# Last chunk of an FFT mixing layer: output transform in two halves of its channels, all its blocks summed in SBUF, three groups of zero matmuls, and a new order of the work

## The chip, the cores and the metric

The kernel runs on one core of a Trainium2 chip. The metric is device time in microseconds (us), as the median of several executions. A profile records one further execution: what each engine did and what it waited for. TensorE is PE (its weight loads PEld), VectorE DVE, ScalarE ACT, GpSimd POOL; SyncE, SP, issues most of the DMA transfers.

## What is computed

A layer over 2048 positions and 640 channels, all float32: a gated blend of a long causal convolution (A) and a spectral filter (B).

```python
def _A_ref(q, k, v, shift_k, ssm_k, ssm_D):
    ...                                   # k_shift: causal convolution of k with 4 taps
    kv = k_shift * v
    L = 2 * S
    ...                                   # kv_f, kf_f: FFTs of length L of kv and of ssm_k
    y_f = kv_f * kf_f[None, :, :, :]
    y = irfft2(y_f, s=(1, L))[:, 0, :S, :]
    y = y + kv * ssm_D[None, None, :]
    return q * y

def _B_ref(x, w_r, w_i):
    X = rfft2(x, axes=(-2, -1)) * (w_r + 1j * w_i)
    return irfft2(X, s=(S, D), axes=(-2, -1))

x = A_q
g = sigmoid((x * gate_w).sum(-1, keepdims=True))
return g * _A_ref(...) + (1 - g) * _B_ref(x, ...)
```

## The kernel before

All Fourier transforms are matmuls with constant matrices, so PE does most of the work; every stage of it is followed by a move out of PSUM on DVE, ACT or POOL. The 2048 positions are held as 128 partitions by 16 blocks n, the 640 channels (permuted) as five chunks c of 128.

**B, the spectral part.** x comes in 16 tiles (L342, "a<-xT"). `fold` (L347 to L358) adds and subtracts quarter tiles on DVE or POOL, with a small copy on ACT (L355). `dfwd` transforms two blocks at a time over the channels (L371, L377), and ACT copies the result into XX (L387 to L394). Then come the transform over positions, first stage `b1` (L437, transposed back by L440), second stage `bs2` (L456) with the filter product (L468, L470) and its sums (L476), and the first inverse stage `i1` (L314 on XX, transposed by L319). The rest is `bfin`, for two blocks at a time: the last inverse stage over positions (L498, L506), a copy (L517), the inverse over channels with the constant "dic" (L525, L530), ACT's scaling by 1 - g (L547 to L550), a combination on DVE (L553), and three sums and differences (L555, L556) that give the 640 output channels of a block.

**A, for each chunk.** `kv` convolves with the taps (L592 and L595, or L601 and L609) and multiplies by v (L632) after eight transposes on PE (L624). The first FFT stage is `s1` (L649, transposed by L652), once for the filter ("a", loaded as h) and once for kv. `amid` is the second stage and the product (L685, then L694, L696, L700, L702); for chunks 2, 3 and 4 its complex parts are summed by `asum` (L709). `is1a` is the first inverse stage in two halves of 64 channels (L314 on ZZ, transposed by L319). `afin` ends a chunk for eight blocks at a time: q is loaded and multiplied by g on ACT (L733), sixteen matmuls over all 128 channels give the last inverse stage (L744), DVE multiplies by q (L751).

**Joining A and B.** For chunks 0 to 3 `afin` writes its eight blocks to the output (L764), and `bout` later adds the spectral part with accumulating DMAs that POOL issues (L570). For the last chunk two ways are used. In blocks 0 to 7, `bout` writes the spectral part first (L568) and `afin` accumulates onto it (L762). In blocks 8 to 15 (`KEEP = (1,)`) the spectral part stays in a buffer of SBUF; POOL adds (L758) and SP writes (L760).

**What sets the order.** Every operation is registered with `op`, with its dependences, buffers and alternatives of engine (`either`). A table of numbers, `TABLE`, gives the order: "51+1/2/3" runs operation 51 in its second alternative, with buffer slots 2 and 3. The engines work through their own instructions in that order, and the numbers of buffers are fixed: eleven "a", five "s", eight banks of PSUM. PE starts with 24 matmuls on a zeroed tile, "wrm" (L773).

Of the kernel before, what the change touches and what calls it, by code (L numbers as in the profile page):

```python
# [25 lines left out]
KEEP = (1,)  # L26
ADDS = {}

TABLE = """
57/0 0 1/0 3 5 2 50/1 145/2 331/0 138/3 339/4 36/5 94/6 58+1/0/1 30/7 101/8 59+1 62/1 61+1 79/9 63 60<61 6 51+1/2/3 55/2 52+1 53+1 56 54+1 146+1/4/0  # L30
64/4/6 150/3 147<146 151 148 149 139/2/4 332/0 333 334 71 143/2 65 66 67 140 340+1 70 144 69 335/10 341/6/0 68 142 141 37/1/3 38 323/0 343/2 72/0
345/1 152/4/0 41 336/2 39 344 40+1<39 167/3 160/4 123/5 342 31+1/2/1 32 35 159 328/7 34 153 33 155 102+1/0/4 154 42+1/2/6 106/0 157 103+1 16/8 105+1
158 156 107 104+1 95+1/2/0 324/0 96+1 116/6 49 80+1/1/3 98+1 48 325 99/4 43 81<98 97 46 10/9 100 45 326 44 108/6/4 47 82 83 84/2 85 73+1/2/1 346 77/3
74+1 75<74 78 349/2 327/0 109 115 168/0/4 110 111 347/4 114 350 76 433/1 113 112 348 405/0 169 86+1/0/2 172/6 225/3 9/0 171 173 170+1 161+1/2/0 162+1
165/7 163+1 219/4 329/4/0 8 124+1/1/3 93 245/0 337/2 164<124 166 87 330 290/10 88 4 125 92 90 338 89 126 174/6/4 91 128/0 129 251/5 127 427/7
117+1/2/1 121/1 118+1 119+1 120+1 351/2/1 181 17/0/4 18 122 19+1<18 21 130/4/0 352 20+1 175 176 11/2/0 177 407/2 178 12 180 15 179 13 409/6 136 131
133 134 132 14 22+1/2/6 137 135 353/0 23 29 27 25 28 357/4 24 355/6 26 184/2 358 406/8 356 411/9 408<14 354 192/4 193 416/0 413/2 410 188/6 182 186/0
189 183 412 185 375/4 187 379/6 383/2 376/1 380/6 377 363/0 378 384/3 381+1 190/4 386 364/9 385 365+1 194/2 191 428+1 382+1 429/4/2 195 366+1 417/6
371/6 372/9 430 434+1 246/2 247/2/0 220/0 204/4 374+1 248 221/4/1 373+1 420/0 418/9 437/2 222 7 249 232/4 202/6 438 250 205 414/0/0 419 203 226/2
359/4 415 227/8 224 264/9 360/3 228/0/2 223 422/2 361 229 493/0 362 435/6 200/0 395/1 231 252/2 436 233/4 230 253/3 201 421 387/6 254/1/4 367/0  # L40
234/3/0 235 388/8 368/2 494/0 198/2 258/4 370 390+1 369 431/4 495/7 196/0 389 432 255<389 496 497/8 303/3 284/5 199 197 499/7 498+1 396 393/4 237<498
504/0 424/8 236 423 391/0 500 394 265/4 400/2 285/6 392 501/7 286/2/0 425/0 256 287 397/2 257 426 266/6 267/3/1 288 506/5 289 259/6 515/8 401 398 268
304/0 439/4/1 399 260/4/0 270 297/6 261 445/2 269 440 212/9 305/4 306/2/1 262 443/6 263 441/4 502/0/0 446 442 307 505/1 507 444 298/2 508/3 291/4
206/4 292/0 299/3/0 503 402/6 308 521/5 309 300 510/7 516+1 471/0 293/4/1 301 455/2 403 459/4 302 472/2 294 404 456/0 474 600/0 473 460/6 463/6 458
296 277/0 457 467/0 464/3 461+1 475/2 465 468/10 466 462 213/6 476/2 451/4 469 214/6 470 452/10 477 295<477 215/2/0 447/0 478 207/6 448/3 454+1<478
517/2/0 449 208/1/4 453+1 488/2 450 519/0 209 604/10 216 518 512/4 481/4 601/8 211+1 520 217<211 602/6 522+1 509+1 483/9 606/3 479/0 603+1 210+1 608/6
589/0 482 511<210 489 605 480 278/4 513/6 279/7 591/1 271/10 514 525/0 218 607 590/4 527/2/1 280/3/1 526 523/6 238/5 533/4 528 611/3 281 529/0 484
584/0 534 592 531/2 272/4 593/7 524 490/6 532 595/1 273/4/0 283 282 594 485/2 530 274 491 239/0 597/10 276 486 240/7 241/2/1 551/4 275 487 543/6 492
552/3 596 559/2 553 544/0 554 547/0 560/4 545 242 561 598/4/0 548/1 562 546 617/9 539/2 540/4 550+1 599 696/0 549 555/6 579/5 243+1 704/7 609/4 675/2
556/10 541 535/0 542 563/2 557+1<542 610 558+1 536/3 564/1 537 538 565+1 623/4/2 627/0 566+1 629/6 624 628 697/8 625/4 630 570 244 320/0 580 569 567  # L50
626 316/4 321 318/0 317 700/4 698/6 319 314/4 571 702/10 315 685/0 568 693/1 585 322/0 574 310/0 612+1 573 572 311 312/4 699 313 577/0 689/6 701 575/4
578 686/4 618+1 613/0/1 576 703 621/2 615/4 687/10 622 619/6 616 691/3 688 586/2 614 581/4 690 620 587 707/9 582 655/0 588 692 583 639/6 656/4 643/2
657 640/0 658 651/4 644/10 641 631/0 713/6 642 632/3 694/6/0 645 984/3 646 854/2/1 634 652/0 666<646 633 695 680/10 654+1 852+1/0/2 855 665 705/6 853
635/2 653+1 706 647/0 636/4 648/4 856/6/4 638+1 650 649 637+1 667 668 800/0/0 857 858/3 869/4 798+1/2/1 859 860 801 664 861 868 870 719/0/0 862 871
663 799 659/6 872 873 802/2/4 720 660/5 874/1 875 661+1 662+1 814 771/0/2 815/0 803 817 876 670 816 773+1/6/1 804/4 818 819 772 725/0 805 806 669 807
774 808 721/2 726 820/8 673/4 681 708+1 863/7 864 722 674 671/0 865 822 866 879/0 672 676 775/4/6 677/0 787 788/3 790 789 776 791 777/1 682/2 778 792
779 793/4 780 678 709/4/2 794 821 781 723/0 823 679 710 782/5 711/6 877 783 724 884+1/4/2 809/9 712 795 885 796 714+1 886/0/0 715/6 683 797 717/4 824
684 887 888/2/0 878 716 810 825/6/3 718 867 784 785 786 890/1 889 811 899 892 813 891 961+1/4/0 826 893 900/2 894 751/6 902 897/2 901 895/6 962 903
727/2 752/4 904 896 755/4 753 907 728/1 754 905/4 731/0 756/8 730 735/6 906 729 732/10 908 758 736/4 757 739/2 738 733+1<757 827/4/2 737 740/1 734+1
959+1/6/1 828 898 766+1 829+1/0/4 960 742 741+1<742 761 963/6/2 842/4 762 841 830 844 843 831/2 765 845 832 846 833 834 934/0/3 847/7 848 965/0 835  # L60
964 974 966 967 936+1/4/1 849 935 968 836/5 850 975/4 977 812 969 747/0 976 760 978 979 937 743/6 748/8 838 938/4/2 837 744/2 970/10 839 746 745 759
971 939 972 911/6/2 749 950/1 840 940/3 949 750 941 952 973 763+1 909+1/0/0 951 912 764+1 851 942 953 767/4 954 910 980/4<764 943 955/1 944 913+1/0/2
880 945/6 981 768 946 956 957 948 914 769/4 915/1 947 916 917 958 918 925/0 924 919 926 983 927 770 985 920/9 982 922 921 928 923 929 930+1/8 881/0
931+1 933 986/4 882 932<931 883 988 987 991+1 989+1 992 990
"""
# [836 lines left out]
```

## Time and profile before

| | |
|---|---|
| median of 3 executions | 289.94 us (288.68 to 290.15) |
| profiled execution | 291.7 us |
| its span, first to last instruction | 289.9 us |
| mean granted clock of TensorE | 0.980 |
| DMA | 53.93 MB, 186 GB/s |

The table and the lines shown in the prediction read as follows. "Busy" is the time in which an engine had an instruction in work. A line of a timeline has the start, the length, the engine, the source line, the operation with its output and inputs, and how often it ran; in square brackets is the idle time before it and what ended it. A line of a group has the total busy time and the mean length of one in nanoseconds. A float32 matmul is two passes in the counts. PEclk is the clock that TensorE was granted, in tenths of full speed for each fortieth of the span. DMA rows have the transfers, KB of each, and the median time from issue to landing.

### The profile page before, as it was taken

What the parts mean: (1) busy time and instruction counts of PE and PEld (TensorE: products, weight loads), DVE (VectorE), ACT (ScalarE), POOL (GpSimd) and SP (SyncE); (2) the same over time, 40 slices, a digit from 0 to 9 for tenths busy, and PEclk for the clock granted to TensorE, in tenths of its full rate; (3) what the DMA queues carried; (4) which work ended last, traced back from release to release, by engine and by line L of the source; (5) the groups of instructions that cost most, each with busy time, mean ns of one, the idle gap of its engine ahead of it and who ended that gap; (6) DMA issues with size and microseconds to landing.
All of it is one profiled execution on the core that took longest, in us unless ns stands there. A gap on an engine that the chain in (4) does not pass through costs nothing.

```text
span 289.9 us, 9390 instructions
## 1 busy us (share of the span) xinstructions
PE 258.9 (89%) x4024; PEld 169.9 (59%) x4024; DVE 225.9 (78%) x284; ACT 151.4 (52%) x315; POOL 205.8 (71%) x206
## 2 busy tenths in 40 slices
PE   8784999989999899889999988999998998999750
PEld 8663797534554366534385323678766775888450
DVE  2689698497999799899999999993467857358670
ACT  2238349715456465756655763354594036486710
POOL 1362732367897998776996999858990876889872
PEclk9899799999999999999999999999999999999996
DMA  7999999370155785847558657292003397305788
GB/s 211 418 394 363 379 339 398 109 290 18 49 183 155 249 235 159 287 119 251 175 186 266 257 154 310 79 270 103 3 3 91 93 196 128 54 22 76 111 114 144
DMA packets 25432, 53.93 MB, mean 186 GB/s; under 512 B 1840, under 2 KB 13360, under 8 KB 24880
## 3 DMA queue, kind: packets, MB, share of 16 engines
q1 hardware_dynamic: 22048, 48.63, 48.9%
q0 software_dynamic: 3344, 4.72, 11.7%
q8 instruction: 31, 0.51, 0.7%
q14 instruction: 9, 0.07, 0.1%
HBM read 43.38 MB, written 9.96 MB: 184 GB/s over the span
## 4 chain that ended last, share of the span: by engine, by line
PE 64%; DVE 22%; issue 5%; ACT 3%; DMA 2%; POOL 1%; POOLq 1%; SPq 1%; ACTq 0%; DVEq 0%
PE banks L685 12%; PE banks L649 9%; PE banks L314 7%; PE banks L530 7%; PE banks L498 6%; PE banks L437 5%; PE banks L744 5%; PE banks L371 4%; DVE ZZ L652 3%; DVE XX L319 3%; DVE ZZ L319 3%; DMA a<-xT 2%; PE banks L525 2%; DVE s L468 2%; DVE ZZ L700 2%
## 5 line engine op out<-in xcount | busy, mean ns | idle before, releaser
L609 POOL TENSOR_TENSOR a<-a,a 128x1024 f32<-128x1024 f32 x21 | 50.1, 2392 | 13.7 <-ACT a L601 10.6
L652 DVE STREAM_TRANSPOSE ZZ<-banks 128x1024 f32<-128x1024 f32 x40 | 47.9, 1229 | 9.0 <-ACT XX L391 4.7
L601 ACT ACTIVATE a<-k,one 128x1024 f32<-128x1024 f32 x32 | 35.9, 1149 | 26.2 <-POOL a L609 9.7
L685 PE MATMUL banks<-ZZ,s2a 64*32 64x256 f32 x1280 | 41.0, 387 | 3.5 <-issue 1.3
L702 POOL TENSOR_TENSOR ZZ<-a 128x512 f32<-128x512 f32 x24 | 30.5, 1288 | 12.1 <-ACT a L694 10.9
L685 PEld LDWEIGHTS banks<-ZZ,s2a 64*32 64x32 f32 x1280 | 23.9, 104 | 17.5 <-issue 4.3
L553 DVE SCALAR_TENSOR_TENSOR s<-banks,om,s 128x322 f32<-128x322 f32 x32 | 17.4, 550 | 21.4 <-ACT s L550 20.9
L700 DVE TENSOR_TENSOR ZZ<-banks,s 128x512 f32<-128x512 f32 x40 | 25.3, 682 | 6.1 <-ACT s L696 5.9
L709 POOL TENSOR_TENSOR ZZ<-ZZ 128x512 f32<-128x512 f32 x21 | 26.4, 1283 | 3.0 <-DVE ZZ L700 2.9
L476 POOL TENSOR_TENSOR XX<-s,s 128x320 f32<-128x320 f32 (+1 forms) x29 | 24.3, 858 | 4.3 <-DVE ZZ L700 2.2
L371 PE MATMUL banks<-dfc,s 128*128 128x162 f32 x128 | 22.7, 335 | 4.9 <-POOL s L350 2.9
L314 PE MATMUL banks<-ZZ,one 32*64 32x512 f32 x448 | 26.6, 607 | 0.3 <-DVE XX L319 0.3
L319 DVE STREAM_TRANSPOSE ZZ<-banks 128x2048 f32<-128x2048 f32 x10 | 22.9, 2306 | 4.0 <-PE banks L314 4.0
L694 ACT ACTIVATE a<-banks 128x1024 f32<-128x1024 f32 x20 | 20.4, 1028 | 10.0 <-PE banks L685 9.0
L371 PEld LDWEIGHTS banks<-dfc,s 128*128 128x128 f32 x128 | 20.4, 211 | 7.6 <-POOL s L350 3.1
L733 ACT ACTIVATE a<-a,g 128x128 f32<-128x128 f32 x80 | 24.3, 391 | 0.9 <-DMA a<-q 0.9
L649 PE MATMUL banks<-a,one 64*128 64x512 f32 x80 | 21.1, 615 | 3.1 <-DVE ZZ L319 1.6
L744 PE MATMUL banks<-ZZ,is2a 128*64 128x128 f32 x320 | 19.5, 277 | 3.1 <-ACT a L733 2.8
L744 PEld LDWEIGHTS banks<-ZZ,is2a 128*64 128x64 f32 x320 | 18.1, 134 | 5.8 <-ACT a L733 3.7
L649 PE MATMUL banks<-kvt,one 64*128 64x512 f32 x80 | 20.0, 616 | 0.2 <-ACT a L694 0.2
L437 PE MATMUL banks<-XX,two 64*128 64x464 f32 (+1 forms) x88 | 19.8, 582 | 0.1
L530 PE MATMUL banks<-dic,s 128*128 128x161 f32 x128 | 19.6, 305 | 0.0
(83 smaller groups left out, 474.9 us busy)
## 6 DMA issues: line engine op xcount, KB each, us to landing
a<-xT SPq DMA_DIRECT2D x16, 512.0 KB, 9.6
k<-k SPq DMA_DIRECT2D x10, 704.0 KB, 5.3
a<-h SPq DMA_DIRECT2D x10, 544.0 KB, 5.1
a<-w SPq DMA_DIRECT2D x16, 322.0 KB, 3.8
a<-v SPq DMA_DIRECT2D x10, 512.0 KB, 5.8
a<-q SPq DMA_DIRECT2D x10, 512.0 KB, 4.9
out_dram<-a SPq DMA_DIRECT2D x8, 512.0 KB, 4.7
out_dram<-a POOLq DMA_DIRECT2D x16, 256.0 KB, 5.9
```

The lines of the kernel that those rows point to most:

```text
L314: mm(p[h * 64:h * 64 + 64, j, :nd * 8], is1[r, c, :], v[r, h * 2 + ri, :, d0:d0 + nd, :].rearrange("p m d e -> p d m e"), start=(i == 0), ...
L319: nc.vector.transpose(by_col(x, d0, nd), p[:, :, :nd * 8].rearrange("p j (d i) -> p d j i", i=8))
L371: mm(v(q)[:, i, :CB], sb(f, 5, 128)[:, x], dfc[:, x], start=first and i == 0, stop=True, skip_group_check=True)
L437: mm(v()[:, b], m1b[r, ri], xv[r, ri, d0:d0 + nd], start=ri == 0, stop=ri == 1)
L530: mm(v(q)[:, i, :161], sb(u, 5, 128)[:, q], dic[:, q * 161:q * 161 + 161], start=first and i == 0, stop=True, skip_group_check=True)
L601: tap = lambda t, j: op([("ACT", act_us(1024), lambda: act(sb(t, 8, 128), K(j), AF.Copy, scale=sh[:, c, j:j + 1]))], r=[k, "one"], w=[t], ...
L609: either(1024, lambda o: o(sb(ts[x], 1024), sb(ts[x], 1024), sb(ts[y], 1024), op=OP.add), r=[ts[y]], w=[ts[x]])
L649: mm(ps(p)[:, b], m1[r], v[r], start=True, stop=True)
L652: op([("DVE", dve(1024), lambda: nc.vector.transpose(by_col(Z(z), u * 32, 32), ps(p).rearrange("p b (d n) -> p d b n", n=16)))], r=[p], w= ...
L685: apart(c, m, "mid", mm(ps(p)[j * 32:j * 32 + 32, h].rearrange("p (y r d) -> p y r d", y=2, r=2)[:, :, ri], s2a[r, k, ri * 32:ri * 32 + 32 ...
L700: alts = [("DVE", dve(512), lambda x=x, dst=dst, hv=hv: tt(dst(), V(part(ps(p), zy)), hv(), op=OP.mult))]
L744: mm(v[b * 64:b * 64 + 64, j, :], is2a[:, n2, :], row(Z(zh), n2), start=True, stop=True)
```

## The change

1. The last chunk no longer uses `afin`. `gated` (taken out of `afin`) loads and scales q for both groups of eight blocks; `alast` then makes the last inverse stage for half of the channels (64) and all 16 blocks, with 32 matmuls of 64 columns a half, and needs only that half's `is1a`.
2. `KEEP = (0, 1)`: the spectral part of the last chunk stays in SBUF for all 16 blocks. `alast` multiplies into an "s" buffer, adds, and SP writes four pieces of 128 x 512. The writes L568 and the accumulating DMA L762 go. The output buffer is split: the first four chunks as before, the last one by halves, so that each partition's piece is one run of 2 KB; the host puts it together.
3. `FILL = 3`: three groups of five matmuls on the zeroed tile.
4. `TABLE` is made anew throughout, with other alternatives of engine and other slots.

```diff
-KEEP = (1,)
+KEEP = (0, 1)
 ADDS = {}
+FILL = 3
...
-57/0 0 1/0 3 5 2 50/1 145/2 331/0 138/3 339/4 36/5 94/6 58+1/0/1 30/7 101/8 59+1 62/1 61+1 79/9 63 60<61 6 51+1/2/3 55/2 52+1 53+1 56 54+1 146+1/4/0
+148/0 6 60/1 5 53/2 342/3 8 326/0 141/4 0 348/5 1/0 39/6 331/7 149+1/0/1 33/8 104/9 150<149 153/1 82/10 152+1 97/0 154 151+1 61+1/2/3 65/2 62+1 63<62
...
+    outs = out[:, :16 * (D - P)].rearrange("p (n c d) -> p n c d", n=16, d=P)
+    outl = out[:, 16 * (D - P):].rearrange("p (s n d) -> p s n d", s=2, n=16)
...
-    def afin(c, zh, n0):
+    def gated(c, n0):
         qt = new("a")
...
+        return qt
+
+    def afin(c, zh, n0):
+        qt = gated(c, n0)
...
+    def alast(zh, qts, dh):
+        unit("afin", NCH - 1, dh)
+        p = new("ps", 2)
+        d = slice(dh * 64, dh * 64 + 64)
+
+        def pe_():
+            v = ps(p).rearrange("p q (j d) -> p (q j) d", d=64)
+            for n in range(16):
+                for b in range(2):
+                    n2 = b * 16 + n
+                    mm(v[b * 64:b * 64 + 64, n, :], is2a[:, n2, :], row(Z(zh), n2)[:, d], start=True, stop=True)
+
+        pe(8 * f32(128), pe_, "128x64", r=[(zh, "f", dh), "is2a"] + qts, w=[p], new=[p], use=[zh])
+        for q, qt in enumerate(qts):
+            t, keep = new("s"), kept[q]
+            op([("DVE", dve(512), lambda q=q, qt=qt, t=t: tt(sb(t, 8, 64), ps(p)[:, q].rearrange("p (j d) -> p j d", d=64), sb(qt, 8, 128)[:, :, d], op=OP.mult))],
+               r=[p, qt], w=[t], new=[t])
+            either(512, lambda o, t=t, keep=keep: o(sb(t, 8, 64), sb(t, 8, 64), sb(keep, 8, 128)[:, :, d], op=OP.add), "DVE",
+                   r=[(keep, n) for n in range(q * 8, q * 8 + 8)], use=[keep], w=[t])
+            load(lambda q=q, t=t: dma(outl[:, dh, q * 8:q * 8 + 8, :], sb(t, 8, 64)), 262, r=[t])
...
+    for i in range(FILL):
+        unit("fill", i)
+        pf = new("ps")
+
+        def fill(pf=pf):
+            for _ in range(5):
+                mm(ps(pf)[:, 0, :128], wrm, wrm, start=True, stop=True)
+
+        pe(1.15, fill, "F", r=["wrm"], w=[pf], new=[pf])
...
+        if c == NCH - 1:
+            for dh in range(2):
+                alast(zh, qts, dh)
```

In the changed program the line numbers are one to a few dozen higher: L371 is L372, L437 L438, L314 L315, L319 L320, L553 L554, L649 L652, L652 L655, L685 L688, L700 L703, L709 L712; L768 is `alast`'s matmul, L773 its product, L775 its sum, L777 its write, and L794 the zero matmuls.

**The start, on PE.** The first rows before; s_ and a_ are buffers of the pools "s" and "a", "dfc" is the constant of `dfwd`:

```order
L773 MATMUL banks<-wrm 128x128 x24
L371 MATMUL banks<-dfc,s_77 128x162 x4
L371 MATMUL banks<-dfc,s_75 128x162 x4
L377 MATMUL banks<-dfc,s_77 128x164 x4
L377 MATMUL banks<-dfc,s_75 128x164 x4
L649 MATMUL banks<-a_67,one 128x512 x4
```

The same place now:

```order
L785 MATMUL banks<-wrm 128x128 x24
L794 MATMUL banks<-wrm 128x128 x5
L652 MATMUL banks<-a_66,one 128x512 x4
L794 MATMUL banks<-wrm 128x128 x5
L372 MATMUL banks<-dfc,s_74 128x162 x4
L372 MATMUL banks<-dfc,s_77 128x162 x4
```

The first filter matmuls (L652) moved ahead of the first spectral pair, with a group of zero matmuls on either side.

**The start, on DVE, at the last fold.** Before, the end of the last fold (L347 to L351) and what follows it:

```order
L347 TENSOR_TENSOR s_76<-a_72 128x512
L348 TENSOR_TENSOR s_76<-a_72 128x256
L358 SCALAR_TENSOR_TENSOR s_74<-s_76,two 128x128
L350 TENSOR_TENSOR s_74<-s_76 128x256
L351 TENSOR_TENSOR s_74<-s_76 128x256
L652 STREAM_TRANSPOSE ZZ<-banks 128x32x16x2 x3
L440 STREAM_TRANSPOSE XX<-banks 128x29x16x2
L405 TENSOR_TENSOR lg<-XX 128x32
```

Now:

```order
L348 TENSOR_TENSOR s_78<-a_71 128x512
L349 TENSOR_TENSOR s_78<-a_71 128x256
L596 SCALAR_TENSOR_TENSOR banks<-k_61,one,banks 128x1024
L357 TENSOR_TENSOR s_75<-s_78,banks 128x128
L596 SCALAR_TENSOR_TENSOR banks<-k_61,one,banks 128x1024
L596 SCALAR_TENSOR_TENSOR a_71<-k_61,one,banks 128x1024
L633 TENSOR_TENSOR kvt_62<-banks,a_69 128x4x2x128
L655 STREAM_TRANSPOSE ZZ<-banks 128x32x16x2
L406 TENSOR_TENSOR lg<-XX 128x32
```

Three tap operations (L596) and a product with v (L633) that stood ahead of the last folds now stand behind them. Ahead of the last fold DVE has two transposes L652 fewer as well, and nine more of the 256-wide additions, which POOL had.

**The end, on PE.** Before, the last `bfin` pair stands between the two halves of the last inverse stage:

```order
L314 MATMUL banks<-ZZ,one 64x512 x16
L530 MATMUL banks<-dic,s_74 128x161 x4
L530 MATMUL banks<-dic,s_76 128x161 x4
L525 MATMUL banks<-dic,s_74 128x163 x4
L525 MATMUL banks<-dic,s_76 128x163 x4
L314 MATMUL banks<-ZZ,one 64x512 x16
L744 MATMUL banks<-ZZ,is2a 64x128 x32
```

Now:

```order
L526 MATMUL banks<-dic,s_75 128x163 x4
L526 MATMUL banks<-dic,s_76 128x163 x4
L531 MATMUL banks<-dic,s_75 128x161 x4
L531 MATMUL banks<-dic,s_76 128x161 x4
L794 MATMUL banks<-wrm 128x128 x5
L315 MATMUL banks<-ZZ,one 64x512 x32
L768 MATMUL banks<-ZZ,is2a 64x64 x64
```

Both halves of the inverse stage moved behind the last pair, with the third group of zero matmuls between.

**The end, on DVE.** Now the last rows are:

```order
L554 SCALAR_TENSOR_TENSOR s_74<-banks,om,s_74 128x322 x2
L554 SCALAR_TENSOR_TENSOR s_75<-banks,om,s_75 128x322 x2
L320 STREAM_TRANSPOSE ZZ<-banks 128x64x16x2
L557 TENSOR_TENSOR a_71<-s_75 128x190
L320 STREAM_TRANSPOSE ZZ<-banks 128x64x16x2
L557 TENSOR_TENSOR a_65<-s_75 128x128
L773 TENSOR_TENSOR s_76<-banks,a_67 128x512
L773 TENSOR_TENSOR s_77<-banks,a_72 128x512
L775 TENSOR_TENSOR s_76<-s_76,a_63 128x512
L773 TENSOR_TENSOR s_74<-banks,a_67 128x512
L773 TENSOR_TENSOR s_75<-banks,a_72 128x512
L775 TENSOR_TENSOR s_74<-s_74,a_63 128x512
```

One more L775 follows on DVE, and the fourth is POOL's last. Before, the two transposes stood between pairs of L553, and L751 ended the list.

104 lines of the change are left out of this document (47 added, 57 removed).

## The prediction

> **What bounds the kernel now.** I read the page first, then the busy time of each engine by stage, then the timelines of the first 60 us and the last 25.
>
> ```profile
> PE 258.9 (89%) x4024; PEld 169.9 (59%) x4024; DVE 225.9 (78%) x284; ACT 151.4 (52%) x315; POOL 205.8 (71%) x206
> PEclk9899799999999999999999999999999999999996
> ```
>
> TensorE is the nearest thing to one bound, but 89% is an average, and its granted clock dips twice early. The stages, with idle time as length less busy time:
>
> ```profile
> 0.00:55.20 55.20, 46.96 (x354) 38.17 (x356) 39.09 (x78) 27.78 (x74) 19.77 (x30) 0.94 0.90 341
> 55.20:100.00 44.80, 43.53 (x720) 21.16 (x716) 39.70 (x42) 21.93 (x32) 36.24 (x27) 1.00 0.44 146
> 100.00:150.00 50.00, 45.69 (x911) 26.82 (x912) 48.76 (x54) 30.13 (x50) 42.65 (x36) 1.00 0.64 201
> 150.00:200.00 50.00, 47.20 (x912) 26.36 (x891) 45.94 (x44) 26.91 (x42) 42.01 (x31) 1.00 0.65 220
> 200.00:250.00 50.00, 47.88 (x740) 35.15 (x737) 32.33 (x40) 25.99 (x65) 35.37 (x47) 1.00 0.39 78
> 250.00:272.00 22.00, 22.00 (x331) 18.24 (x337) 12.54 (x19) 14.16 (x40) 20.09 (x28) 1.00 0.39 58
> 272.00:290.00 18.00, 5.68 (x96) 4.04 (x80) 7.59 (x10) 4.53 (x16) 9.64 (x12) 0.87 0.87 129
> ```
>
> The columns are length, then PE, weight loads, DVE, ACT, POOL busy, then clock, DMA share, GB/s. Three limits follow one another. The start has DMA at 0.90 and DVE in a chain; from 100 to 200 DVE is busy 94.7 us of 100 and PE idles 4.3 and 2.8; from 200 on PE leads. In the last 18 us PE works 5.7. PE's losses are therefore at the start, some 10.5 us spread from 55 to 250 (1.3, 4.3, 2.8, 2.1), and 12.3 at the end.
>
> **The end.** Times are the start, then the length.
>
> ```profile
> 266.58 2.08 PE L314 MATMUL banks<-ZZ,one 32*64 32x512 f32 x32
> 270.99 0.84 PE L525 MATMUL banks<-dic,s 32*128 32x163 f32 x16
> 273.13 1.14 DVE L553 SCALAR_TENSOR_TENSOR s<-banks,om,s 128x322 f32<-128x322 f32 x2 [2.02 <-ACT s L550]
> 273.50 0.73 ACT L550 ACTIVATE s<-banks,bio,om 128x81 f32<-128x81 f32 x2
> 274.19 2.31 DVE L319 STREAM_TRANSPOSE ZZ<-banks 128x2048 f32<-128x2048 f32 x1
> 276.64 3.85 PE L744 MATMUL banks<-ZZ,is2a 128*64 128x128 f32 x64 [2.81 <-ACT a L733]
> 281.37 2.95 POOL L758 TENSOR_TENSOR a<-a,a 128x512 f32<-128x512 f32 x2
> L760 SPq DMA_DIRECT2D out_dram<-a x2: 383/576/769, 283.1 to 284.3; - x2
> DMA to landing us min/median/max: 4.3/4.5/4.8
> ```
>
> Call T the end of the last spectral ("dic") matmuls, 271.8 here. The last output leaves at 284.3, lands 4.5 later at 288.8, and the span ends 1.1 after that. T to the end is 18.1 us; the other half of the last inverse stage stood 2.1 ahead of it, and in the new program both halves stand behind T. Like for like, before needs 20.2.
>
> The new last piece, from T (in the order that the rows of the section on the change have): zero matmuls to +1.6 (10 passes at 7.68/48 us, the warm row below), first inverse half to +3.7. DVE first does two pairs of L554: ACT finishes at 274.23, which is T+2.4, so the second pair ends at +3.5, and that also frees the banks of the second inverse half (done +5.8). Transpose +3.7 to +6.0, a subtraction (0.35), transpose +6.4 to +8.7, another to +9.0. The first half of L768 runs from +6.0, the second from +8.7 or later. DVE then: two products, one addition, two products once the second half is done, two additions, each 0.68 as L700 has it. Last, a transfer of 256 KB and the 1.1.
>
> ```profile
> 257.04 0.66 PE L506 MATMUL banks<-c,XX 128*32 128x64 f32 x32
> L556 DVE TENSOR_TENSOR a<-s 128x190 f32<-128x190 f32 x1 | 0.3, 350 | 0.0
> L700 DVE TENSOR_TENSOR ZZ<-banks,s 128x512 f32<-128x512 f32 x40 | 25.3, 682 | 6.1 <-ACT s L696 5.9
> a<-w SPq DMA_DIRECT2D x16, 322.0 KB, 3.8
> out_dram<-a SPq DMA_DIRECT2D x8, 64.0 KB, 2.3
> ```
>
> Two prices are not in the trace. Each L768 half has 64 passes over 64 columns with 64 columns of weights. If columns count, it is half of L744: 1.9. If passes count, it is L744 whole: 3.85, 60 ns a pass. L506, the only 64-column row, takes 20 ns a pass with half the weight columns; doubled that is 40 ns, 2.6 us, my value, the nearest row. The transfer writes 2 KB runs where L760 wrote 512 B: at most L760's 4.8, at least the 64 KB row's 2.3; I take 3.8, the row nearest in size. So the second half ends at +11.3, the additions at +14.1, landing at +17.9, end +19.0: **1.2 us gained**. With both low it is +17.3 (2.9 gained), with both high +22.4 (2.2 lost). The removed 512 KB accumulating transfer, the eight small writes and the halved gating wait (L733 to L744, 2.81) are in this sum: no term of their own.
>
> The Trainium skill, "TensorE: Matmul & The Clock Gate", section "Back-to-back issue gap", speaks against narrower matmuls: from 1 to 64 columns it gives no gain, and ≈62 ns per matmul where the sequencer decodes it. By that a half would be 4.0 us and the end some 22. L506's 20 ns a pass disagrees, L744's 60 agrees by chance or not; it is the first rival.
>
> **The start.**
>
> ```profile
> 1.06 7.68 PE L773 MATMUL banks<-wrm 128*128 128x128 f32 x48 [1.06 <-DVE wrm L768]
> 10.75 3.81 PE L371 MATMUL banks<-dfc,s 128*128 128x162 f32 x16 [2.01 <-DVE s L350]
> 29.00 4.14 PE L371 MATMUL banks<-dfc,s 128*128 128x162 f32 x16 [2.88 <-POOL s L350]
> 37.10 2.47 PE L371 MATMUL banks<-dfc,s 128*128 128x162 f32 x16
> 52.28 2.89 PE L649 MATMUL banks<-kvt,one 64*128 64x512 f32 x12
> 55.01 5.55 PE L437 MATMUL banks<-XX,two 64*128 64x464 f32 x26
> 13.00:14.00 1.00, 1.00 (x5) 1.00 (x5) 0.55 (x1) 0.41 (x1) 1.00 (x2) 0.50 1.02 419
> 30.00:31.00 1.00, 1.00 (x5) 1.00 (x5) 1.00 (x4) 0.11 (x1) 0.31 (x1) 0.50 1.02 418
> 49.32 0.41 DVE L351 TENSOR_TENSOR s<-s 128x256 f32<-128x256 f32 x1
> 54.42 3.51 DVE L652 STREAM_TRANSPOSE ZZ<-banks 128x1024 f32<-128x1024 f32 x3 [4.69 <-ACT XX L391]
> ```
>
> After waits of 2.01 and 2.88 the granted clock is 0.50, and the same sixteen passes take 3.81 and 4.14 instead of 2.47: 3.0 us. The first zero matmuls fill the gap after the warm-up, the second stand between the first chunk matmuls and the first spectral pair. A group costs 1.6, but only where PE had work. The first stands where PE waited 2.01; the second waits behind data that come in the order x, h, dfc, and if that cover is gone it costs its 1.6. I count nothing for them and don't add the 3.0 either: it lies inside the stretch whose end DVE sets, next.
>
> The Trainium skill, same page, section "What's actually happening", drops the clock after an idle window of about 3.4 us; a 2.0 us gap would then be harmless and the first zeros useless. The trace differs: 2.01 us sufficed.
>
> DVE decides the rest. Ahead of its last fold (ending 49.7) the new order has two L652, three L595 and one L632 fewer, and nine quarter-tile additions more.
>
> ```profile
> L652 DVE STREAM_TRANSPOSE ZZ<-banks 128x1024 f32<-128x1024 f32 x40 | 47.9, 1229 | 9.0 <-ACT XX L391 4.7
> L595 DVE SCALAR_TENSOR_TENSOR banks<-k,one,banks 128x1024 f32<-128x1024 f32 x4 | 5.1, 1286 | 0.9 <-ACT banks L592 0.8
> L632 DVE TENSOR_TENSOR kvt<-banks,a 128x1024 f32<-128x1024 f32 x10 | 12.0, 1209 | 1.8 <-PE banks L624 1.8
> L350 DVE TENSOR_TENSOR s<-s 128x256 f32<-128x256 f32 x8 | 3.4, 419 | 0.2
> ```
>
> That is -2.5 -3.9 -1.2 +3.8, or 3.8 less: last fold at 45.9. From the old last fold to L437 it was 5.3. PE now has the six kvt matmuls (2.9) out of that gap and three groups of about 1.0 in it (eight transposes, two chunk matmuls, two more; 2.89 for six gives 0.96 for two). So L438 starts at 45.9 + 5.3 - 2.9 + 3.0 = 51.3 instead of 55.0: 3.7 earlier, with 2.9 of work still owed. For PE that is 0.8. For DVE it is more: the 4.69 in which it waited for ACT is now filled with the deferred L595 and L632, which stand right behind the last fold, and the next stage is DVE's. If all of it is filled the gain is 4.7. I take **2.4 us**, a little below the middle of 0.8 and 4.7, as the DMA share of 0.90 can hold up the folds; the bounds are 0 (the loads bind) and 4.7.
>
> **The middle.**
>
> ```profile
> 165.66 11.63 DVE L319 STREAM_TRANSPOSE XX<-banks 128x1728 f32<-128x1728 f32 x6
> L609 DVE TENSOR_TENSOR a<-a,a 128x1024 f32<-128x1024 f32 x3 | 3.5, 1209 | 0.5 <-POOL a L609 0.5
> L476 DVE TENSOR_TENSOR XX<-s,s 128x322 f32<-128x322 f32 x3 | 1.4, 483 | 0.0
> ```
>
> Ahead of this, after which the spectral output can run, DVE now has 7 L652, 2 L632, 12 L700 and 3 L609 fewer; with the small ones (two L476 of 0.5 fewer, one L471 of 0.8, by its width from L609, and ten fold operations of 0.4 more) -8.6 -2.4 -8.2 -3.6 -1.0 +0.8 +3.8, some 19 us less. PE has less ahead of it too (256 instead of 384 matmuls of L685, 14 fewer of L649, 16 fewer of L624), so both arrive there sooner. The stage that DVE bounds ends 19 us earlier, and in it PE idles 8.4 us in 145 (55 to 200): **1.1 us gained**, if the deferred work finds room later. The bounds are 5.6 lost and 5.2 gained, the two rivals on it.
>
> **Sum:** 1.2 + 2.4 + 1.1 = 4.7. The profiled execution took 291.7 (span 289.9): 287.0. The median of the runs, 289.94, is 1.8 below it, so I predict 285.2.
>
> **Rivals.**
> 1. A pass costs L744's 60 ns whatever its width: L768 then ends the tail at +21.4, 2.4 later, 287.6. For it L744, against it L506. Chance 0.14.
> 2. The change doesn't do in the start what its zeros are for: PE still goes idle behind the loads, the clock drops as before, or the DMA share of 0.90 sets the pace. The start gives nothing: 287.6. Chance 0.14; with the first together 290.0.
> 3. Slower: DVE becomes full after the spectral inverse. Over the whole program its work grows by some 9 us (six L709 sums priced as L700, the ten fold operations, the kept sums of the end, less the L609); with the 19 deferred, 28 more stand behind that point. From 150 to 272 it is free 4.1 + 17.7 + 9.5 = 31. Up to 31 they hide; beyond, or where DVE stands in order behind a wait for ACT, PE waits as from 100 to 150, 4.3 in 50, over 122 us: 10.5 instead of 4.9, so 5.6 lost in place of 1.1 gained. 289.9 - 1.2 - 2.4 + 5.6 = 291.9. For it: 28 is close to 31, and L553 already waits 2.02 for ACT in the end's rows. Against: the stage starts 19 us earlier, so there is more room. Chance 0.18.
> 4. The balance is better than I count: half of the 10.5 us idle from 55 to 250 goes: 5.2 instead of 1.1, 281.1. Chance 0.11.
>
> **How the numbers follow.** My case has 0.43 and its own range 282.5 to 288.0. The range of 8 in 10 reaches from beneath the fourth to the third, 280.5 to 291.5. Half a per cent of 289.94, about what a measurement can tell, is 1.45. Faster, below 288.5: nearly all of my case, the fourth, most of rivals 1 and 2: 0.67. Within: 0.17. Slower: most of the third, 0.16.
>
> **What would show it.** First spectral matmuls at 2.5 us per sixteen passes and clock 1.00 to 40 us; the first L438 near 51; the inverse XX transposes (L320) near 145 to 150; L768 at 2.6 a half; the last L777 within 15 us of the last L531. Wrong would be: L438 after 54, PE idle over 8 us between 150 and 270, or L768 at 60 ns a pass.

## The result, and the profile after

| | before | after |
|---|---|---|
| median | 290.04 us (4 runs) | 286.4 us (4 runs, 285.73 to 286.73) |
| ratio, 95% interval | | 0.9873 (0.9845 to 0.99) |
| profiled execution, span | 291.7, 289.9 | 286.16, 284.4 |

The change saves 3.6 us in the median, 1.3%. Four slow executions beside the experiments, three of the kernel before (293.3, 293.5 and 366.8 us) and the profiled one of run c (637.5), are in no median, ratio or interval. The page of the changed kernel, its busy row and its clock:

```profile
PE 262.1 (92%) x4118; PEld 174.0 (61%) x4118; DVE 232.2 (82%) x307; ACT 150.8 (53%) x315; POOL 191.8 (67%) x185
PEclk9999999999999999999999999999999999999998
```

Its stages (length, then PE, weight loads, DVE, ACT, POOL busy, clock, DMA share, GB/s):

```profile
0.00:55.20 55.20, 47.38 (x382) 38.44 (x384) 43.46 (x92) 33.56 (x82) 20.00 (x23) 1.00 0.88 329
55.20:100.00 44.80, 43.63 (x759) 22.17 (x756) 37.92 (x39) 16.39 (x25) 38.62 (x31) 1.00 0.56 183
100.00:150.00 50.00, 47.77 (x948) 27.46 (x948) 48.38 (x50) 29.65 (x49) 42.73 (x36) 1.00 0.66 212
150.00:200.00 50.00, 46.94 (x846) 27.97 (x846) 44.58 (x50) 28.98 (x50) 34.03 (x22) 1.00 0.48 166
200.00:250.00 50.00, 49.23 (x707) 36.69 (x704) 34.38 (x42) 26.54 (x70) 31.28 (x42) 1.00 0.38 83
```

Both dips of the clock are gone, and PE's idle time from 55.2 to 250 fell from 10.5 to 7.2. From the timeline, the start and the end (the last row is that of the four writes of L777):

```profile
8.66 1.28 PE L794 MATMUL banks<-wrm 128*128 128x128 f32 x10
13.90 2.37 PE L372 MATMUL banks<-dfc,s 128*128 128x162 f32 x16
50.88 1.85 PE L438 MATMUL banks<-XX,two 64*128 64x464 f32 x8
265.35 2.47 PE L531 MATMUL banks<-dic,s 128*128 128x161 f32 x16
268.86 2.05 PE L315 MATMUL banks<-ZZ,one 32*64 32x512 f32 x32
271.05 2.32 DVE L320 STREAM_TRANSPOSE ZZ<-banks 128x2048 f32<-128x2048 f32 x1
273.53 2.31 DVE L320 STREAM_TRANSPOSE ZZ<-banks 128x2048 f32<-128x2048 f32 x1
275.89 2.10 PE L768 MATMUL banks<-ZZ,is2a 128*64 128x64 f32 x64 [0.36 <-DVE ZZ L320]
277.12 0.68 DVE L775 TENSOR_TENSOR s<-s,a 128x512 f32<-128x512 f32 x1
277.72 1.28 DVE L773 TENSOR_TENSOR s<-banks,a 128x512 f32<-128x512 f32 x2
278.92 1.47 DVE L775 TENSOR_TENSOR s<-s,a 128x512 f32<-128x512 f32 x2
DMA to landing us min/median/max: 2.7/2.8/3.5
```

T, the end of the last spectral matmuls, is 267.8, and from T to the end, the tail, it is 16.6. The kernel before has 20.2 like for like, from 269.8 (its T of 271.8 less the inverse half of 2.1 that stood ahead of it). In these two traces the tail is 3.6 shorter and T is 2.0 earlier. The second L768 half ends at 278.0 while DVE, without a gap since 275.93, is still at its products: in this trace DVE's sum of operations leads to the writes. The last write is issued at T + 12.6 instead of T + 14.6 and lands in 2.8 instead of 4.3 us. Landing is counted from the start of an issue.

### The profile page after: what moved, and what is told of

Its sections match the earlier page's. It is cut to its first block, busy times and chain, and to the rows that moved or that the text cites. A ratio compares the mean times of both kernels' runs of the same rounds, so it can differ in the third digit from the quotient of the medians.

```text
span 284.4 us, 9580 instructions
## 1 busy us (share of the span) xinstructions
PE 262.1 (92%) x4118; PEld 174.0 (61%) x4118; DVE 232.2 (82%) x307; ACT 150.8 (53%) x315; POOL 191.8 (67%) x185
## 4 chain that ended last, share of the span: by engine, by line
PE 62%; DVE 18%; DMA 6%; issue 5%; ACT 4%; POOL 2%; SPq 1%; DVEq 1%; ACTq 0%
PE banks L688 11%; PE banks L652 9%; PE banks L315 7%; PE banks L438 7%; PE banks L531 6%; PE banks L499 6%; DVE ZZ L320 4%; PE banks L752 4%; DMA a<-h 3%; PE banks L457 3%; DMA dfc<-dfc 3%; PE banks L625 2%; PE banks L526 2%; DVE s L469 2%; DVE XX L320 2%
## 5 line engine op out<-in xcount | busy, mean ns | idle before, releaser
L610 POOL TENSOR_TENSOR a<-a,a 128x1024 f32<-128x1024 f32 x24 | 56.9, 2376 | 10.9 <-ACT a L602 9.3
L655 DVE STREAM_TRANSPOSE ZZ<-banks 128x1024 f32<-128x1024 f32 x40 | 48.0, 1225 | 3.1 <-PE banks L652 2.9
L688 PE MATMUL banks<-ZZ,s2a 64*32 64x256 f32 x1280 | 41.5, 388 | 2.2 <-issue 1.3
L697 ACT ACTIVATE a<-banks 128x1024 f32<-128x1024 f32 x20 | 20.3, 1026 | 26.3 <-PE banks L688 25.7
L688 PEld LDWEIGHTS banks<-ZZ,s2a 64*32 64x32 f32 x1280 | 24.0, 104 | 15.6 <-issue 3.4
L703 DVE TENSOR_TENSOR ZZ<-banks,s 128x512 f32<-128x512 f32 x40 | 25.5, 684 | 6.1 <-ACT s L699 5.8
L315 PE MATMUL banks<-ZZ,one 32*64 32x512 f32 x448 | 27.4, 606 | 0.3 <-DVE s L554 0.3
L320 DVE STREAM_TRANSPOSE ZZ<-banks 128x2048 f32<-128x2048 f32 x10 | 22.9, 2309 | 4.9 <-PE banks L315 4.6
L477 POOL TENSOR_TENSOR XX<-s,s 128x322 f32<-128x322 f32 (+1 forms) x31 | 25.8, 855 | 1.4 <-DVE ZZ L703 0.8
L554 DVE SCALAR_TENSOR_TENSOR s<-banks,om,s 128x322 f32<-128x322 f32 x32 | 17.1, 546 | 10.0 <-ACT s L551 9.4
L712 POOL TENSOR_TENSOR ZZ<-ZZ 128x512 f32<-128x512 f32 x15 | 19.0, 1282 | 7.7 <-DVE ZZ L703 4.8
L652 PE MATMUL banks<-a,one 64*128 64x512 f32 x80 | 21.3, 625 | 1.9 <-DVE a L663 0.8
L557 POOL TENSOR_TENSOR a<-s 128x128 f32<-128x128 f32 (+1 forms) x27 | 14.8, 561 | 11.5 <-DVE s L554 10.6
L372 PE MATMUL banks<-dfc,s 128*128 128x162 f32 x128 | 19.5, 304 | 2.8 <-ACT banks L356 2.8
L652 PE MATMUL banks<-kvt,one 64*128 64x512 f32 x80 | 20.3, 617 | 1.5 <-DVE ZZ L320 0.8
L531 PE MATMUL banks<-dic,s 128*128 128x161 f32 x128 | 19.9, 306 | 0.8 <-DVE ZZ L320 0.6
L372 PEld LDWEIGHTS banks<-dfc,s 128*128 128x128 f32 x128 | 17.8, 189 | 3.9 <-ACT banks L356 1.9
L531 PEld LDWEIGHTS banks<-dic,s 128*128 128x128 f32 x128 | 17.8, 190 | 3.4 <-DVE ZZ L320 1.6
L315 PEld LDWEIGHTS banks<-ZZ,one 32*64 32x64 f32 x448 | 11.5, 129 | 13.6 <-issue 11.3
```

What stands on the lines that cost most here:

```text
L315: mm(p[h * 64:h * 64 + 64, j, :nd * 8], is1[r, c, :], v[r, h * 2 + ri, :, d0:d0 + nd, :].rearrange("p m d e -> p d m e"), start=(i == 0), ...
L320: nc.vector.transpose(by_col(x, d0, nd), p[:, :, :nd * 8].rearrange("p j (d i) -> p d j i", i=8))
L372: mm(v(q)[:, i, :CB], sb(f, 5, 128)[:, x], dfc[:, x], start=first and i == 0, stop=True, skip_group_check=True)
L477: either(2 * nc_, lambda q, ri=ri, o=o, dst=dst: q(dst(), T(t1)[:, :, ri], T(t2)[:, :, 1 - ri], op=o), r=[t1, t2], w=[("XXp", z, i, ri)])
L531: mm(v(q)[:, i, :161], sb(u, 5, 128)[:, q], dic[:, q * 161:q * 161 + 161], start=first and i == 0, stop=True, skip_group_check=True)
L610: either(1024, lambda o: o(sb(ts[x], 1024), sb(ts[x], 1024), sb(ts[y], 1024), op=OP.add), r=[ts[y]], w=[ts[x]])
```

## The experiments

Each kernel was timed in five rounds beside the kernel before; ratios are to that. e1 to e4 were timed together, so were c, e5, e6 and e7, and e8, e9 and e10. c is the changed kernel again; 286.4 within 0.5 was expected of it, and it took 286.6. All line numbers are the kernel's own and may be one or a few off those above.

| run | order | median | ratio (95%) | first L437/L438 | T | T to end |
|---|---|---|---|---|---|---|
| first profiles: before | old | 290.0 | | 55.0 | 269.8 | 20.2 |
| after | new | 286.4 | 0.9873 | 50.9 | 267.8 | 16.6 |
| e9, before again | old | 290.0 | 0.9976 (0.995 to 1.0003) | 53.6 | 267.5 | 19.9 |
| c, changed again | new | 286.6 | 0.9883 (0.9839 to 0.9926) | | | |
| e1, no start zeros | new | 287.5 | 0.9915 (0.9886 to 0.9944) | 50.7 | 267.2 | 17.7 |
| e2, no last zeros | new | 286.7 | 0.9895 (0.9868 to 0.9923) | 51.2 | 268.7 | 17.0 |
| e3, halves together | new | 288.3 | 0.9954 (0.9929 to 0.9979) | 50.9 | 267.9 | 17.7 |
| e4, short runs | new | 288.1 | 0.9932 (0.9906 to 0.9958) | 50.7 | 267.6 | 17.9 |
| e7, DVE relieved | new | 287.2 | 0.9915 (0.9883 to 0.9947) | 50.8 | 266.7 | 17.2 |
| e6, zeros alone | old | 290.6 | 1.002 (0.9988 to 1.0052) | 51.9 | 265.7 | 20.6 |
| e10, e6 again | old | 290.4 | 1.0017 (0.9983 to 1.005) | 52.3 | 267.0 | 20.3 |
| e5, new tail | old | 286.1 | 0.9864 (0.9819 to 0.991) | 55.0 | 267.7 | 17.3 |
| e8, new tail and zeros | old | 286.2 | 0.9859 (0.9824 to 0.9895) | 53.5 | 269.1 | 17.1 |
| e11, e5 with accumulating write | old | 289.0 | 0.9963 (0.9929 to 0.9997) | 54.6 | 267.0 | 19.9 |

T in the old order is always given less the 2.07 of the inverse half ahead of it. For c there are times alone.

**e1.** The first two groups of zero matmuls are left out, they compute nothing that is used:

```diff
+ZEROS = (0, 5, 0)
...
-            for _ in range(5):
+            for _ in range(ZEROS[i]):
```

> The changed kernel without its first two groups of zero matmuls (order and tail kept). Theory A, the zeros hold the clock and the clock is on the path: PE waits 2.0 us behind the warm-up, the granted clock falls to 0.50 as in the kernel before, the first sixteen spectral passes take 3.8 instead of 2.4 us, the first L438 comes 1.3 us later than 50.88 and the run takes 287.7. Theory B, the zeros hold the clock but DVE sets the start: the same slow sixteen passes, L438 at 50.9 within 0.3, the run 286.4 within 0.4. Theory C, the zeros do nothing: clock 1.00 at 13 us without them too, 286.4.

The timeline of e1 on PE:

```profile
10.60 1.99 PE L653 MATMUL banks<-a,one 64*128 64x512 f32 x8 [1.43 <-DVE a L664]
13.40 2.44 PE L373 MATMUL banks<-dfc,s 128*128 128x162 f32 x16 [0.81 <-POOL s L352]
50.71 1.85 PE L439 MATMUL banks<-XX,two 64*128 64x464 f32 x8
```

Theory C for the trace: the new order has split the long wait into 1.43 and 0.81, and the clock stays at 1.00 without zeros. T is no later. The median, though, is nearer to theory A's 287.7 than to C's 286.4: it is 0.8 over that of e2, which was timed beside it and has these zeros, and 0.8 over that of c. The intervals overlap, so a worth of up to about 1 us is neither shown nor ruled out.

**e2.** `ZEROS = (5, 0, 5)`, the last group left out.

> The changed kernel without its last group of zero matmuls. The first L315 can then start at the end of the last spectral matmuls (T) instead of 1.1 us later, and PE waits some 1.4 us for the second, whose banks L554 frees at T + 3.3. Theory A, this wait lowers the clock: the second L315 and both L768 halves take up to twice as long (2.1 to 4.2 us each), T to the end 18.6 to 20.7 instead of 16.6, the run 288 to 290. Theory B, 1.4 us are too short for that, and the first transpose stands in DVE's order behind L554 in any case: T to the end 16.6, 286.4 within 0.4. Theory C, the zeros are only in the way: T to the end 15.5, 285.3.

Its timeline:

```profile
268.58 2.82 PE L316 MATMUL banks<-ZZ,one 32*64 32x512 f32 x32
272.00 2.05 PE L316 MATMUL banks<-ZZ,one 32*64 32x512 f32 x32 [0.61 <-DVE s L555]
```

Theory B. The first inverse half starts at T but ends at T + 2.75, against T + 3.1 with the zeros, and the transposes stand at T + 3.2 in both. The second half, behind a wait of 0.61, takes 2.05 as with the zeros. T to the end is 17.0 instead of 16.6 because the writes landed in 3.3 instead of 2.8.

**e3.** The first L768 half waits for both transposes. The cut shows one entry of TABLE; "<771" adds the wait for operation 771.

```diff
-... 985/0 ...
+... 985/0<771 ...
```

> The changed kernel, but the first half of the last output transform (L768) also waits for the transpose of the other half, as a transform in halves of blocks has to. If the overlap of the first half with the second transpose is what shortens the tail, both halves stand behind 275.85: T to the end grows from 16.6 by 2.1 us (one half of 2.10), the run takes 288.5. If the additions in SBUF and the writes set the end whatever the halves do (DVE's four products and additions follow one another), the growth is under 1.0 us.

From e3's timeline, both halves in one row:

```profile
276.00 3.95 PE L768 MATMUL banks<-ZZ,is2a 128*64 128x64 f32 x128 [2.67 <-DVE ZZ L320]
279.56 2.91 SPq L779 DMA_DIRECT2D out_dram<-s  x4
```

The first theory: the writes begin at T + 11.6 instead of T + 10.1, and the median is 1.9 over 286.4 and 1.6 over that of e2, timed beside it. The tail in this trace grew only by 1.1 because the writes landed in 2.3 instead of 2.8.

**e4.** The last chunk in another order in the output array.

```diff
-    outl = out[:, 16 * (D - P):].rearrange("p (s n d) -> p s n d", s=2, n=16)
+    outl = out[:, 16 * (D - P):].rearrange("p (n s d) -> p s n d", s=2, n=16)
```

> The changed kernel with its last output written in runs of 256 bytes instead of 2 KB (the output array holds the last chunk in another order). If the length of the runs sets the landing, the last four writes land in 4.5 to 4.8 us as L760's 512-byte runs of the kernel before did, instead of 2.7 to 3.5: T to the end grows by 1.0 to 2.0 us, the run takes 287.4 to 288.4. If the landing is set by the size (256 KB each) or by a fixed cost, it stays at 2.8 and the run at 286.4 within 0.4.

e4's four writes (lengths of the issues, min, median and max in ns, when the first and the last began, then landing):

```profile
L777 SPq DMA_DIRECT2D out_dram<-s x4: 373/578/1139, 277.6 to 280.5; - x4
DMA to landing us min/median/max: 3.2/3.7/3.9
```

The median is 1.7 over 286.4 and 1.4 over that of e2, timed beside it, as the first theory has it. In the trace something else stands out: an issue takes up to 1.14 us, where the changed kernel's takes 0.33, so that the last one ends 1.1 later from T. The landing of 3.7 contains this length, and it lies within what 2 KB runs show from one execution to the next (2.3 in e3, 4.0 in e1). So the longer issue is the likely reason; one trace doesn't show it.

**e5.** The old order, without zeros, with the new tail: TABLE of the kernel before, with the operations of its last `afin` replaced by those of `alast`, the early writes L568 taken out, and the freed "k" buffer for the kept sums of blocks 0 to 7.

> The order of the kernel before, without zero matmuls, with the new last transform alone: halves of channels, all last-chunk additions in SBUF, eight early writes less, last output in 2 KB runs. Theory A, as predicted (tail 1.2, start and order 3.5 of the gain): the run takes 288.6. Theory B, as the trace of the changed kernel reads (tail 3.6, end of the last spectral matmuls 1.95 earlier): 288.3 less what the tail gains more, 287 to 288. Theory C, the order gives nothing at all, the tail everything: the second transpose ends where it did in the kernel before (276.5), 8.65 us to the end follow as in the changed kernel, a span of 285.2 and a run of 285 to 286.4.

Its timeline:

```profile
16.29 3.62 PE L653 MATMUL banks<-a,one 64*128 64x512 f32 x8 [2.14 <-POOL a L664]
29.09 3.97 PE L372 MATMUL banks<-dfc,s 128*128 128x162 f32 x16 [2.88 <-POOL s L351]
55.03 6.80 PE L438 MATMUL banks<-XX,two 64*128 64x464 f32 x32
268.96 0.84 PE L527 MATMUL banks<-dic,s 32*128 32x163 f32 x16
```

Theory C. The start has the old order, L438 at 55.03 and two slow spells, yet T is where the changed kernel has it (267.7 against 267.8), and the run is as fast as c (286.1 and 286.6 beside each other). The first spell is not where the first profile has it: it hit eight filter passes (3.62 instead of 1.99) behind a wait of 2.14. The figures of 3.81 and 4.14 in the expectation of e8 are those of the first profile, not of e5. The reverse, the new order with the old tail, was not run.

**e6 and e10.** The kernel before with zeros: `WARM = 30`, and nine in the spectral pair of blocks 8 and 9.

```diff
         def pe_(turn):
+            for _ in range(9 if ns[0] == 8 else 0):
+                mm(ps(p[0])[:, 0, :128], wrm, wrm, start=True, stop=True)
```

> The kernel before with zero matmuls alone: six more in the warm-up and nine ahead of the spectral pair at 29.0, so that PE is not idle for 2.0 and 2.9 us there; nothing else is changed. Both slow spells should go: sixteen passes at 2.4 to 2.5 us instead of 3.81 and 4.14. Theory A, the clock is on the path: 3.0 us less, 286.8. Theory B, DVE sets the end of the start: the first L437 at 55.0 within 0.4 and the run 289.8 within 0.5.

> e6 again (kernel before with fifteen zero matmuls), for a second profile: e6's profiled execution took 288.1, its eleven others 289.5 to 291.8. If the profile was a lucky execution, this one takes 290 to 291 and its trace shows what was lucky: the first L437 later than 51.9, or the middle or the landing longer. If the zeros are worth 3 us, the median is 287.

e6's timeline, then e10's:

```profile
27.66 2.37 PE L371 MATMUL banks<-dfc,s 128*128 128x162 f32 x16
51.90 6.80 PE L439 MATMUL banks<-XX,two 64*128 64x464 f32 x32
```

```profile
PEclk9999999999999999999999999999999999999976
52.34 6.79 PE L439 MATMUL banks<-XX,two 64*128 64x464 f32 x32
PE banks L458 <- issue: 1.3, 1, 1.3
268.25 0.84 PE L527 MATMUL banks<-dic,s 32*128 32x163 f32 x16
273.90 5.45 PE L746 MATMUL banks<-ZZ,is2a 128*64 128x128 f32 x64 [2.81 <-ACT a L735]
```

By the medians of both sets the run gains nothing, as theory B has it, though not by its reason: in both traces the zeros hold the clock at the start, and L439 comes 1.2 (e10) to 1.7 (e6) earlier than in e9. At T e10 has 0.5 left of it and then loses 1.6 in the last transform, where its clock falls; e6 has 1.7, but its profiled execution, 288.1, is the only one of its twelve below 289.4. Of the others there is no trace, but their granted clock is on record; the part on the zeros below reads it.

**e9.** The kernel before, unaltered.

> The kernel before, unaltered, for a second profile. Its first profiled execution took 291.7, 1.7 over its median, and had one wait of 1.31 us of L685 at 246.08 that no instruction released; e5 and e6, in the same order, have none there. If that wait is a mishap of one execution, it is missing here, the last spectral matmuls end 1.3 to 2.0 us earlier than 271.8 and the profiled run is 290 within 0.8. If it belongs to the kernel, it stands there again. The two slow spells of the start should be there in both cases, if the median holds them.

Its timeline:

```profile
10.06 2.73 PE L371 MATMUL banks<-dfc,s 128*128 128x162 f32 x16 [0.48 <-DVE s L350]
27.54 4.14 PE L371 MATMUL banks<-dfc,s 128*128 128x162 f32 x16 [2.88 <-POOL s L350]
53.55 6.79 PE L437 MATMUL banks<-XX,two 64*128 64x464 f32 x32
274.37 3.85 PE L744 MATMUL banks<-ZZ,is2a 128*64 128x128 f32 x64 [2.81 <-ACT a L733]
```

The first slow spell belongs to single executions: here the warm-up ended 0.9 later and the first fold came 0.7 earlier, which leaves a wait of 0.48 and a full clock; only the second spell is there. The longest wait of PE without a releaser is 0.7 instead of 1.31. T is 2.3 earlier than in the first profile, which the prediction took its sum from.

**e8.** e5 with the zeros of e6.

> The old order with the new last transform (as in e5) and with the fifteen zero matmuls of e6. e5's trace has the two slow spells (3.81 and 4.14 us a sixteen) and L438 at 55.03, its runs 286.1. Theory A, the clock in the start is worth what e6's one profile showed (first L437 3.1 us earlier, end of the last spectral matmuls earlier by as much): 283.0 to 283.5, which would beat both kernels. Theory B, as e6's eleven other runs had it, nothing of it is left in the time: 286.1 within 0.7; then the trace must show where the 3 us go.

The start of e8 on PE:

```profile
16.16 2.72 PE L655 MATMUL banks<-a,one 64*128 64x512 f32 x8 [2.13 <-POOL a L666]
53.49 6.80 PE L440 MATMUL banks<-XX,two 64*128 64x464 f32 x32
```

Theory B: 286.2, as e5. In this execution the clock dropped at another wait, of 2.13, and one wait of 1.3 without a releaser came in the middle as in e10. So this trace can't show what a clock held all through is worth. The six executions took 285.1 to 288.0; the fastest has the highest granted clock, 0.994, and is still behind theory A's 283.5.

**e11.** e5 with blocks 0 to 7 of the last chunk written early and accumulated in the output array again. Cuts, against e5:

```diff
-KEEP = (0, 1)
+KEEP = (1,)
...
+                op([("POOL", 1.0, lambda q=q, t=t: nc.gpsimd.dma_start(outl[:, dh, q * 8:q * 8 + 8, :], sb(t, 8, 64), accum_op=OP.add))],
```

> e5 (old order, new last transform in halves of channels), but with the last chunk's first eight blocks added in the output array as in the kernel before, by a POOL-queue accumulating write for each half, with the eight early writes back; the other eight blocks are added in SBUF. If the additions in SBUF carry a share of the gain, the last accumulating write is issued some 0.9 us behind the last product (near T + 10) and lands 6.4 to 6.9 us later as in the kernel before, against 2.7 for a plain write issued at T + 11.4: T to the end 17 to 18 instead of 15.2, the run 288.2. If it is hidden (DVE has two additions of 0.68 less and so ends earlier), T to the end stays within 0.7 of 15.2 and the run at 286.2.

From e11's timeline and its DMA issues (KB each, median to landing):

```profile
278.64 1.51 POOL L780 DMA_DIRECT2D out_dram<-s  x1
279.35 0.94 SPq L778 DMA_DIRECT2D out_dram<-s  x2
out_dram<-s POOLq DMA_DIRECT2D x2, 256.0 KB, 6.3
out_dram<-s SPq DMA_DIRECT2D x2, 256.0 KB, 5.2
```

The first theory: T to the end 19.9 instead of 17.3 (the expectation counts it without the inverse half of 2.1), the median 2.9 higher (ratios of 0.9963 and 0.9864). The accumulating write lands in 6.3, and the plain writes beside it in 5.2 instead of 2.9.

**e7.** The changed kernel without zeros; of the last four products POOL makes one, from a copy that ACT takes, and POOL also has its sum and one subtraction L557. A cut:

```diff
+            if dh and q:
+                op([("ACT", 0.6, lambda t=t, src=src: act(sb(t, 8, 64), src(), AF.Copy))], r=[p], w=[t], new=[t])
+                op([("POOL", 1.3, lambda qt=qt, t=t: ptt(sb(t, 8, 64), sb(t, 8, 64), sb(qt, 8, 128)[:, :, d], op=OP.mult))], r=[qt], w=[t])
```

> The changed kernel with DVE relieved between the last transposes and the end, and without any zero matmuls: one of the four products is made by POOL from a copy that ACT takes out of the bank, its addition by POOL too, and the 190-column subtraction L557 between the transposes by POOL. In the changed kernel DVE is busy from the second transpose (275.75) to the last addition (280.39) without a gap, while the second half of L768 ends at 278.0. If DVE sets the end there, it does 0.32 + 0.64 less: T to the end 15.6 instead of 16.6, the run 285.4. If POOL (some 3.7 us behind 276.0) is late instead, or sharing the port makes both slower, the end stays at 16.6: 286.4.

e7's timeline:

```profile
275.10 1.81 POOL L777 TENSOR_TENSOR s<-s,a 128x512 f32<-128x512 f32 x1
275.31 2.15 DVE L781 TENSOR_TENSOR s<-s,a 128x512 f32<-128x512 f32 x1
```

The second theory: DVE was spared 0.96, and lost 1.47 in one addition, which took 2.15 beside POOL's product instead of 0.68. The additions end at T + 13.2 instead of T + 12.6, and the run is no faster (287.2 beside 286.6 of c). So DVE's lead in the tail is read from the trace, and this run couldn't confirm it.

## Why the prediction came out as it did

The time was 286.4 against a forecast of 285.2, well in its range, but that is luck: the parts were wrong and made up for one another. 1.2 for the tail and 3.5 for start and middle were forecast; the tail gave all of the gain that the runs can tell. e5 shows it: with the new tail in the old order it is as fast as the changed kernel. From the far ends of the intervals of e5 (0.991) and c (0.9839) the order is worth 0.7% at most, 2.1 us, and not 3.5.

**The tail: right in its mechanism, the terms too dear.** Forecast 1.2, in the first two traces 3.6, in the old order 2.6 to 2.9 (e5 against e9 and before; medians 3.9, interval 2.6 to 5.2). Over all traces T to the end is 19.9 to 20.6 with the old tail and 16.6 to 17.7 with the new one (after, e1, e2, e5, e8). The last write is issued at T + 12.6 (T + 13.2 in e5 and e8) instead of T + 14.6, which is 1.4 to 2.0; the rest is its landing, which differs from one execution to the next. L768 took 2.10 a half, 33 ns a pass, where 2.6 was taken from L506: the price by columns (1.9) was nearer. The section "Back-to-back issue gap" on the Trainium skill's page "TensorE: Matmul & The Clock Gate" gives ≈62 ns a matmul up to 64 columns where the sequencer decodes it; this trace, with 33, does not agree. Landing was 2.8 instead of 3.8, and the zeros and the first inverse half ended at T + 3.1 instead of + 3.7. So the second half of L768 ended at T + 10.2 instead of + 11.3, and the additions at + 12.6 instead of + 14.1. e3, e4 and e11 price the parts: overlapping halves 1.6 to 1.9, 2 KB runs against 256 bytes 1.4 to 1.7, sums in SBUF 2.9. They are not to be added up, as each counts only where it is last. The kernel before wrote runs of 512 bytes, and what 2 KB runs save against those was not tried.

**The start: the early L438 came, the gain did not.** L438 was forecast at 51.3 and came at 50.88, by two errors that cancel: DVE's last fold ended at 43.7 instead of 45.9, and L438 followed 7.2 later instead of 5.4. Sixteen passes took 2.4 and the clock stood at 1.00. From the early L438 the prediction took 2.4, as "for DVE it is more" than PE's 0.8. That is the step that failed. The table shows it: L437/L438 stands at 50.7 to 51.2 in the new order and at 51.9 to 55.0 (mean 53.7) in the old one, and the means of T are 267.6 and 267.7. An L438 that starts early because other work was put behind it is no gain. DVE did fill much of its wait, as forecast, with 43.46 us of work by 55.2 instead of 39.09, but its whole work grew from 225.9 to 232.2, and T did not move. By 55.2 the new program's PE had done 37.0 us of work that counts (47.38 less 7.77 of warm-up and 2.66 of zeros), the old one 36.3 (46.96 less 7.68 and 3.0 of slow spells): 0.7, about PE's share in the prediction. But in e9 the old program had done 37.5 (47.65 less 8.53 and the 1.67 of its one spell), so even the 0.7 is no more than its spread:

```profile
0.00:55.20 55.20, 47.65 (x360) 38.14 (x362) 40.68 (x79) 29.34 (x76) 20.97 (x31) 0.97 0.88 341
```

**The zeros: counted at nothing, and worth nothing that the medians show,** at the start (e1, e6, e10, e8) and at the end (e2). It was right not to add the 3.0 us of slow spells, but the reason, that they lie inside the stretch whose end DVE sets, holds only in part: with the clock held at the start, the old order reaches L439 1.2 to 1.7 earlier, and its median is the same. Besides, one of the two spells was missing in e9.

This does not make the clock worthless. Of the kernel before, 92 executions (e9 and those beside the experiments) have a granted clock on record: the 51 at 0.966 to 0.977 have a median of 290.6, the 41 at 0.978 to 0.987 one of 289.1. With the zeros of e6 and e10 it is 291.3 at 0.978 to 0.983 (14) and 289.9 at 0.985 to 0.993 (10). The difference of some 1.5 is near the 1.6 that e10's last transform lost when the clock fell behind its wait of 2.81. The new tail has no such wait (0.36 ahead of L768 in the changed kernel), so part of what it saves can be this spell. That is an estimate from these numbers; which spell the executions without a trace had is not shown.

**The middle: the milestone and the idle time went as forecast, the time did not.** The inverse XX transposes (L320), forecast near 145 to 150, began at 144.1 instead of 165.7:

```profile
L320 DVE STREAM_TRANSPOSE XX<-banks x6: 1941/1951/1984, 144.1 to 153.8; 128x1728 f32<-128x1728 f32 x3, 128x1696 f32<-128x1696 f32 x3
```

PE's idle time from 55.2 to T is 7.2 after and 8.3 in e5: 1.1 less, the number forecast, though against e9 (9.0) and the first profile (10.5) it is 1.7 and 3.3 less. But PE was busy 205.4, instead of 204.2 in e5 and 203.3 in e9 (both less the 2.07), with nearly the same work left. Two groups of after, then of e5 (busy, mean ns):

```profile
L315 PE MATMUL banks<-ZZ,one 32*64 32x512 f32 x448 | 27.4, 606 | 0.3 <-DVE s L554 0.3
L507 PE MATMUL banks<-c,XX 128*32 128x64 f32 x256 | 6.3, 224 | 0.0
```

```profile
L315 PE MATMUL banks<-ZZ,one 32*64 32x512 f32 x448 | 26.7, 607 | 0.3 <-DVE XX L320 0.3
L508 PE MATMUL banks<-c,XX 128*32 128x64 f32 x256 | 5.6, 223 | 0.0
```

Count and mean are the same within 1 ns, the busy time is 0.7 longer in each: fewer of them overlap. The new order changes more often between kinds of matmul, which would do that; it was not tried by itself and stays open.

**The rivals.** The first fell: a pass of L768 costs 33 ns. The second, that the start gives nothing, came true, though not for its reasons (the clock was held, and L438 came early with the DMA share at 0.88). The third, DVE full late in the program, did not: PE idles 3.8 from 150 to 250 in the new order, 4.9 before, and DVE's work grew by 6.3 instead of 9. The fourth fell with the start.

**The sum** was made against an execution of 291.7. e9's took 289.2, with T 2.3 earlier, so the 2.0 between the two first traces at T lies within the spread of the old program and is no sign of the change. The prediction took 1.8 off the level for this, but read its stages from that execution, idle times and slow spells included.

## What to carry to other kernels

Ask of an earlier milestone what was put behind it, and compare the work done by a fixed time instead; a deferred operation is paid for on the engine that is the bound. What stands behind the last spectral matmuls was different here: an overlap (e3), longer runs (e4) and additions taken out of an accumulating transfer (e11) all showed in the time, each as far as it was last; relieving DVE at the cost of POOL (e7) did not. And take a second profile of the kernel before, before stalls of 1 to 2 us in one execution are priced as its own: here the tail alone, in the old order, is as fast as the whole change.
